# Cached decode attention with a gMLP gate: two blocks of w_out by three smaller transfers, and one group of chunks on a PSUM bank of its own

## The chip, the cores and the metric

One core of one Trainium2 chip. The metric is the device time of one execution in microseconds (us), the median of several runs.

## The reference

One decode step for 8 sequences with 512 features: an attention block over a cache of 4096 positions (32 query heads, 8 key/value heads of 128), multiplied by a gate from a gated MLP, added to the input.

```python
x = A_x                                   # [8, 1, 512]
xn = layernorm(x)
# attention: q = xn @ wq, softmax(q k^T / sqrt(128)) v over 4096 cached positions, then @ wo
s = A(xn, A_k_cache, A_v_cache, A_wq, A_wo)
# gMLP: z = gelu(xn @ w_in) [8, 1792]; z1, z2 = halves of 896; z2 = layernorm(z2)
#       g = w_sp * z2 + b_sp;  B = (z1 * g) @ w_out      (w_out is [896, 512])
g = silu(B(xn, B_w_in, B_w_sp, B_b_sp, B_w_out))
return x + s * g
```

All data are float32. The caches are 2 x 134 MB, so nearly all of the bytes are read once and used once.

## The kernel before

SBUF holds a ring of three slots of 8 MB (64 KB in each of 128 partitions). The first slot takes the MLP's weights (`mlp_slot`), the second `wq`, and from then on the slots take in turn the halves of the key cache (`load_k`, L295) and of the value cache (`load_v`, L302), one half per head, four sequences each. Every one of these loads is issued from the SP queue, in program order, and waits there until the slot that it overwrites has been read by TensorE. The last slot takes `wo` in seven pieces that get smaller (`WO_PIECES`, L319). So the SP queue holds the order: MLP weights (L62), extra w_out rows (L64), `wq` (L76), first half of the keys of head 0, second half of the keys of head 0 (into `mlp_slot`, so it waits for the MLP), then values, and so on.

The work on the engines goes in the same order. `mlp()` computes the gate at the start; `project_q` makes the queries; then, for each of 8 heads, `scores` (L240) for both halves, `softmax`, and `values` (L282) with `combine` (L291) for each sequence. At the end `wo` is multiplied (L333, L342), the gate applied, the input added, and the result stored.

In the MLP, w_in and w_out are cut into blocks of 128 rows. w_out has seven blocks. Five of them (`MAIN`) come with w_in in one transfer over all 128 partitions. The other two (`LOW`, blocks 1 and 3) come by a transfer of their own, `w_low`: each block is cut into 6 chunks of 24 rows (`CH` chunks of `QR` rows, the last chunk has 8), and the chunks lie in 24 partitions, 6 groups (`LOW_E`) of 4 rows (`LOW_R`). In DRAM each of the 6 groups is one stretch, followed by 64 numbers of padding, so that the transfer keeps an outer dimension of 6:

```python
nc.sync.dma_start(mlp_slot[:QR, n_mlp:n_low],
                  w_low[:, :LOW_R * N_LOW].rearrange("e (i n) -> e i n", n=N_LOW))
```

At the end of the MLP the product z1 * g (`u[:, 1]`) is transposed: two transposes of 128 columns for `MAIN` (L181, copied at L182 to `hT`), six of up to 24 columns for `LOW` (L188, copied at L192 to `hL`). Then 17 matmuls (L201; the profile has two records for each float32 matmul of this kind) multiply with the blocks and chunks of w_out. Matmul i goes to group i % 4 of 32 output partitions, all into one PSUM bank, `pw`. L202 copies it, L205 adds the four groups, and L207 to L211 make the gate. `xn`, the layer norm of the input, `hL`'s neighbour `hT` and the copy `y_sb` lie in small buffers; `xn` takes a part of `mlp_slot`.

Of the kernel before, what the change touches and what calls it, by code (L numbers as in the profile page):

```python
# [8 lines left out]
F32 = mybir.dt.float32  # L9
# [4 lines left out]
P = 128  # L14
B, D = 8, 512
HKV, REP, S, DH = 8, 4, 4096, 128
NK = D // P
G = 4
J = S // (G * P)
R = 32  # L20
FH = 896
FQ = 256
NB = FH // P
# [4 lines left out]
SLOT = HALF * UNIT  # L28
WO_PIECES = [(0, 8), (8, 16), (16, 24), (24, 28), (28, 30), (30, 31), (31, 32)]
FOLDED = 16  # L30
LOW_E, LOW_R = 6, 4
QR = LOW_E * LOW_R
CH = -(-P // QR)
MAIN = [0, 2, 4, 6, 5]
LOW = [1, 3]
N_LOW = len(LOW) * CH * D


@with_exitstack
def tile_gqa_gmlp_decode(ctx: ExitStack, tc: tile.TileContext, x, side, kT, v, wq, wo,  # L40
                         w_mlp, w_low, out):
    nc = tc.nc
    const = ctx.enter_context(tc.tile_pool(name="const", bufs=1))
    ring = ctx.enter_context(tc.tile_pool(name="ring", bufs=3))
    work = ctx.enter_context(tc.tile_pool(name="work", bufs=1))
# [4 lines left out]
    def slot():  # L50
        return ring.tile([P, SLOT], F32, name="slot")
# [6 lines left out]

    mlp_slot = slot()
    n_in, n_mlp = NK * 2 * FH, NK * 2 * FH + len(MAIN) * D  # L60
    n_low = n_mlp + N_LOW
    nc.sync.dma_start(mlp_slot[:, :n_mlp], w_mlp)  # L62
    w_in_sb = mlp_slot[:, :n_in].rearrange("p (k n) -> p k n", k=NK)
    nc.sync.dma_start(mlp_slot[:QR, n_mlp:n_low],  # L64
                      w_low[:, :LOW_R * N_LOW].rearrange("e (i n) -> e i n", n=N_LOW))
    w_out_sb = mlp_slot[:, n_in:n_mlp].rearrange("p (j d) -> p j d", d=D)
    w_low_sb = mlp_slot[:QR, n_mlp:n_low].rearrange("p (j a d) -> p j a d", a=CH, d=D)
    spare = [n_low]

    def from_slot(rows, n):  # L70
        lo = spare[0]
        spare[0] = lo + n
        return mlp_slot[:rows, lo:lo + n]
# [6 lines left out]
    ident = const.tile([P, P], F32, name="ident")  # L80
# [20 lines left out]
    sc = ps_fix.tile([P, 2, 512], F32, name="sc")  # L101
# [5 lines left out]
    def scratch(shape, name):  # L107
        t = ps.tile([P, 512], F32, name="scr")
        n = 1
        for s in shape[1:]:  # L110
            n *= s
        return t[:shape[0], :n]
# [2 lines left out]
    st = small.tile([B, 6], F32, name="st")  # L115
    mv = small.tile([B, 2], F32, name="mv")
    rstd = small.tile([B, 2], F32, name="rstd")
    xn = from_slot(B, D)
    nc.vector.bn_stats(st, x_sb)  # L119
    nc.vector.bn_aggr(mv, st)  # L120
    nc.vector.tensor_scalar(rstd[:, 0:1], mv[:, 1:2], EPS, None, op0=ALU.add)
# [9 lines left out]
    def mlp():  # L131
        zu = work.tile([P, 4, FQ], F32, name="zu", tag="p")
        z, u = zu[:, :2], zu[:, 2:]
        hy = work.tile([P, 2 * D], F32, name="hy", tag="pT")
        hT = hy[:, :2 * P].rearrange("p (a s) -> p a s", a=2)
        hL = hy[:QR, 2 * P:2 * P + CH * P].rearrange("p (a s) -> p a s", a=CH)
        y_sb, e = zu[:, :2].rearrange("p a f -> p (a f)"), zu[:, 2, :P]
        pz = scratch([P, 2 * FQ], "pz")
        nc.vector.memset(pz, 0.0)
        for part in range(2):  # L140
            for k in range(NK):
                for g in range(G):
                    lo = g * FQ
                    n = min(FQ, FH - lo)
                    nc.tensor.matmul(pz[R * g:R * (g + 1), part * FQ:part * FQ + n], xnT[:, k, :],  # L145
                                     w_in_sb[:, k, part * FH + lo:part * FH + lo + n],
                                     start=(k == 0), stop=(k == NK - 1))
        zf, uf = z.rearrange("p a f -> p (a f)"), u.rearrange("p a f -> p (a f)")
        nc.vector.tensor_copy(zf, pz)
        nc.vector.tensor_mul(uf, zf, zf)  # L150
        nc.vector.tensor_scalar(uf, uf, 0.044715, 1.0, op0=ALU.mult, op1=ALU.add)
        nc.vector.tensor_mul(uf, uf, zf)
        nc.scalar.activation(uf, uf, AF.Tanh, scale=GELU_C)
        nc.vector.tensor_scalar(uf, uf, 1.0, 0.5, op0=ALU.add, op1=ALU.mult)
        nc.vector.tensor_mul(zf, uf, zf)

        def mean(src, name):
            part_sum = small.tile([P, 1], F32, name="part_sum")
            nc.vector.tensor_reduce(part_sum, src, op=ALU.add, axis=AX.X)
            pm = scratch([P, 1], "pm")  # L160
            nc.tensor.matmul(pm, same_all, part_sum, start=True, stop=True)
            t = small.tile([P, 1], F32, name=name)
            nc.vector.tensor_scalar(t, pm, 1.0 / FH, None, op0=ALU.mult)
            return t

        z1, z2 = z[:, 0, :], z[:, 1, :]
        mu = mean(z2, "mu")
        nc.vector.tensor_scalar(z2, z2, mu, None, op0=ALU.subtract)
        nc.vector.tensor_mul(u[:, 0, :], z2, z2)
        nc.vector.memset(u[(G - 1) * R:, 0, FH - (G - 1) * FQ:], 0.0)  # L170
        var = mean(u[:, 0, :], "var")
        nc.vector.tensor_scalar(var, var, EPS, None, op0=ALU.add)
        rs = small.tile([P, 1], F32, name="rs")
        nc.gpsimd.tensor_tensor(rs, var, neg_half, op=ALU.pow)
        nc.vector.tensor_scalar(z2, z2, rs, None, op0=ALU.mult)
        nc.vector.tensor_scalar(z2, z2, side_sb[:, P:P + 1], side_sb[:, P + 1:P + 2],
                                op0=ALU.mult, op1=ALU.add)
        nc.vector.tensor_mul(u[:, 1, :], z2, z1)
        th = scratch([P, 2 * P], "th")
        for a in range(2):  # L180
            nc.tensor.transpose(th[:, a * P:(a + 1) * P], u[:, 1, a * P:(a + 1) * P], ident)  # L181
        nc.vector.tensor_copy(hT.rearrange("p a s -> p (a s)"), th)  # L182
        for lo in range(0, CH, 4):
            n = min(4, CH - lo)
            tl = scratch([QR, n * P], "tl")
            for a in range(lo, lo + n):
                k = min(QR, P - a * QR)
                nc.tensor.transpose(tl[:k, (a - lo) * P:(a - lo + 1) * P],  # L188
                                    u[:, 1, P + a * QR:P + a * QR + k], ident)
            for a in range(lo, lo + n):  # L190
                k = min(QR, P - a * QR)
                nc.vector.tensor_copy(hL[:k, a], tl[:k, (a - lo) * P:(a - lo + 1) * P])  # L192
        pw = scratch([P, D], "pw")
        todo = [(hT[:, j % 2, R * (j // 2):R * (j // 2 + 1)], w_out_sb[:, i, :]) for i, j in enumerate(MAIN)]
        for a in range(CH):
            k = min(QR, P - a * QR)
            todo += [(hL[:k, a, R * (j // 2):R * (j // 2 + 1)], w_low_sb[:k, i, a, :])
                     for i, j in enumerate(LOW)]
        for i, (lhsT, rhs) in enumerate(todo):
            g = i % G  # L200
            nc.tensor.matmul(pw[R * g:R * (g + 1), :], lhsT, rhs, start=(i < G), stop=(i + G >= len(todo)))  # L201
        nc.vector.tensor_copy(y_sb, pw)  # L202
        py = scratch([P, P], "py")
        for g in range(G):
            nc.tensor.matmul(py[R * g:R * (g + 1), :], same[:, 0, :], y_sb[:, g * P:(g + 1) * P],  # L205
                             start=True, stop=True)
        nc.vector.tensor_scalar(e, py, -1.0, 87.0, op0=ALU.mult, op1=ALU.min)  # L207
        nc.scalar.activation(e, e, AF.Exp)
        nc.vector.tensor_scalar(e, e, 1.0, None, op0=ALU.add)
        nc.vector.reciprocal(e, e)  # L210
        nc.vector.tensor_mul(gate, py, e)  # L211
# [86 lines left out]
    def load_v(h, half, parts):  # L298
# [4 lines left out]
        return t.rearrange("p (i j e) -> p i j e", i=HALF, j=J)  # L303

    mlp()
    project_q(0)
    project_q(1)
    for h in range(HKV):
        for half in range(2):
            scores(h, half, load_k(h, half))  # L310
        pT = softmax(h)
# [18 lines left out]
    part, acc = sc[:, 0, :], sc[:, 1, :P]  # L330
    for m in range(FOLDED):
        h, r = divmod(m, REP)
        nc.tensor.matmul(part[R * r:R * r + B, :], oT[:, h, r, :], wo_sb[:, m, :],  # L333
                         start=(m < REP), stop=(m >= FOLDED - REP))
# [11 lines left out]
    for g in range(G):  # L346
        nc.tensor.matmul(acc[R * g:R * g + B, :], same[:, 0, :B], part_sb[:, g * P:(g + 1) * P],
                         start=False, stop=False)
# [47 lines left out]
```

## Time and profile before

| what | value |
|---|---|
| median of 3 runs | 685.41 us (685.33 to 686.46) |
| the profiled execution | 685.31 us, its span 683.5 us |
| mean granted TensorE clock | 0.763 |
| DMA queue q1 (all loads of SP) | 6510 packets, 290.85 MB |
| HBM read | 290.87 MB, 426 GB/s over the span |

The profile is of one execution. The span runs from the first to the last instruction; the rest of the profiled execution's time lies around it. "DMA share" is the mean busy share of the core's 16 DMA engines; a row of windows gives it for a stretch of time, in microseconds from the span's start. In the chain of waits each row has a start, a length and what released the next. In groups and timeline, `out<-in` names what is written and read, x is a count, and the bracket says how long the engine was idle before and which instruction or transfer ended that.

### The profile page before, as it was taken

Reading aid. Unit: us, or ns where it says so; the run is one execution under the profiler, and the core shown is the slowest. Engines: PE = TensorE matmul, PEld = TensorE weight load, DVE = VectorE, ACT = ScalarE, POOL = GpSimd, SP = SyncE. Lnnn points to the kernel's source line nnn. Section 1 sums busy time; section 2 is a strip of 40 time slices with the busy share of each in tenths; the row PEclk is TensorE's granted clock in tenths of the full one; section 3 lists DMA queues with packets and bytes.
Section 4 is the critical chain, followed back from the end, with each engine's and each line's share of the span. In section 5 each row is a group of like instructions: output and inputs, shape, how many; then the busy total and the mean of one; then the engine's idle time right before and its main releaser. Section 6 shows DMA issues by size and latency. Waiting matters only on the chain.

```text
span 683.5 us, 5757 instructions
## 1 busy us (share of the span) xinstructions
PE 373.0 (55%) x2634; PEld 115.1 (17%) x2634; DVE 168.0 (25%) x272; ACT 13.5 (2%) x27; POOL 3.9 (1%) x11
## 2 busy tenths in 40 slices
PE   1486454446665455556754454555754455645665
PEld 0221121112111111111211021111211121111222
DVE  2420032402430023401431024401422024400350
ACT  0000000000000000000000000000000000000000
POOL 1000000000000000000000000000000000000000
PEclk9778777767778777777787767767777777777788
DMA  9999999999999999999999999999999999999995
GB/s 396 438 430 427 430 442 426 438 433 434 433 427 445 430 433 433 427 427 433 430 437 430 437 430 434 430 430 433 430 430 438 430 434 437 434 430 438 404 427 238
DMA packets 6693, 291.29 MB, mean 426 GB/s; under 512 B 750, under 2 KB 1006, under 8 KB 1398
## 3 DMA queue, kind: packets, MB, share of 16 engines
q1 hardware_dynamic: 6510, 290.85, 98.7%
q8 instruction: 20, 0.33, 0.2%
q10 hardware_dynamic: 160, 0.08, 0.1%
q14 instruction: 3, 0.02, 0.0%
HBM read 290.87 MB, written 0.07 MB: 426 GB/s over the span
## 4 chain that ended last, share of the span: by engine, by line
DMA 80%; PE 15%; issue 4%; DVE 1%; SPq 0%; POOLq 0%; POOL 0%
DMA slot<-in_kT 41%; DMA slot<-in_v 35%; PE sc L240 8%; PE o_ps L282 5%; DMA slot<-in_wo 4%; PE scr L201 1%; PE po_ps L291 0%; DMA x_sb<-in_x 0%; DVE o_sb L287 0%; PE scr L188 0%; SPq L302 0%; DVE hy L192 0%; DVE o_all L285 0%; DVE st L119 0%; PE scr L181 0%
## 5 line engine op out<-in xcount | busy, mean ns | idle before, releaser
L240 PE MATMUL sc<-slot,qz 128*32 128x512 f32 x1024 | 144.1, 726 | 136.1 <-DMA slot<-in_kT 136.1
L282 PE MATMUL o_ps<-slot,pT 128*16 128x512 f32 x1024 | 151.0, 730 | 79.2 <-DMA slot<-in_v 79.2
L285 DVE TENSOR_TENSOR o_all<-o_ps,diag 128x512 f32<-128x512 f32 x64 | 44.3, 692 | 154.2 <-PE o_ps L282 153.7
L245 DVE TENSOR_REDUCE nm<-sc 128x1 f32<-128x1024 f32 x8 | 9.8, 1225 | 278.7 <-PE sc L240 278.7
L240 PEld LDWEIGHTS sc<-slot,qz 128*32 128x32 f32 x1024 | 35.5, 131 | 238.3 <-DMA slot<-in_kT 139.5
L287 DVE TENSOR_REDUCE o_sb<-o_all 128x128 f32<-128x512 f32 x64 | 67.7, 1059 | 2.2
L282 PEld LDWEIGHTS o_ps<-slot,pT 128*16 128x16 f32 x1024 | 29.5, 111 | 159.0 <-issue 108.2
L291 PE MATMUL po_ps<-fold,o_sb 128*128 128x4 f32 x128 | 24.9, 264 | 27.7 <-DVE o_sb L287 27.5
L291 PEld LDWEIGHTS po_ps<-fold,o_sb 128*128 128x128 f32 x128 | 19.2, 189 | 72.5 <-DVE o_sb L287 72.5
L271 PE MATMUL scr<-ident,p 128*128 128x128 f32 x64 | 14.8, 410 | 10.7 <-DVE p L266 10.7
L247 ACT ACTIVATE p<-sc,nm 128x1024 f32<-128x1024 f32 x8 | 8.9, 1114 | 577.4 <-DVE nm L245 577.4
L271 PEld LDWEIGHTS scr<-ident,p 128*128 128x128 f32 x64 | 11.9, 212 | 11.1 <-issue 11.1
L272 DVE COPY pT<-scr 128x512 f32<-128x512 f32 x16 | 11.1, 692 | 10.8 <-PE scr L271 10.8
L145 PE MATMUL scr<-slot,xnT 128*32 128x256 f32 (+1 forms) x64 | 6.4, 547 | 9.6 <-DMA slot<-in_w_mlp 9.6
L218 PE MATMUL scr<-slot,xnT 128*32 128x512 f32 x64 | 8.6, 684 | 0.0
L250 PE MATMUL scr<-ident,nm 128*1 128x128 f32 x8 | 2.2, 270 | 10.9 <-DVE nm L245 10.9
L263 PE MATMUL scr<-wl,same 128*128 128x1 f32 x16 | 3.2, 272 | 6.2 <-DVE wl L261 6.2
L201 PE MATMUL scr<-slot,hy 24*32 24x512 f32 (+2 forms) x34 | 6.2, 726 | 0.5 <-DVE hy L192 0.5
L342 PE MATMUL sc<-slot,oT 128*8 128x128 f32 x128 | 4.4, 273 | 3.8 <-DMA slot<-in_wo 3.8
L266 DVE TENSOR_SCALAR p<-p,w 128x1024 f32<-128x1024 f32 x8 | 6.0, 753 | 0.3
L145 PEld LDWEIGHTS scr<-slot,xnT 128*32 128x32 f32 x64 | 3.4, 161 | 12.2 <-issue 12.1
L333 PE MATMUL sc<-slot,oT 128*8 128x512 f32 x32 | 5.2, 785 | 0.0
(84 smaller groups left out, 62.8 us busy)
## 6 DMA issues: line engine op xcount, KB each, us to landing
slot<-in_v SPq DMA_DIRECT2D x4, 2048.0 KB, 41.9
slot<-in_wo SPq DMA_DIRECT2D x3, 2048.0 KB, 41.5
slot<-in_w_mlp SPq DMA_DIRECT2D x1, 4864.0 KB, 14.6
slot<-in_wo SPq DMA_DIRECT2D x1, 1024.0 KB
slot<-in_w_low SPq DMA_DIRECT2D x1, 576.0 KB
slot<-in_wo SPq DMA_DIRECT2D x1, 512.0 KB, 33.1
slot<-in_wo SPq DMA_DIRECT2D x2, 256.0 KB, 26.7
slot<-in_kT SPq DMA_DIRECT2D x16, 48.5
```

The source lines that it names most:

```text
L145: nc.tensor.matmul(pz[R * g:R * (g + 1), part * FQ:part * FQ + n], xnT[:, k, :], w_in_sb[:, k, part * FH + lo:part * FH + lo + n], start=( ...
L201: nc.tensor.matmul(pw[R * g:R * (g + 1), :], lhsT, rhs, start=(i < G), stop=(i + G >= len(todo)))
L218: nc.tensor.matmul(pq[R * g:R * (g + 1), :], xnT[:, k, :], wq_sb[:, k, lo:lo + REP * DH], start=(k == 0), stop=(k == NK - 1))
L240: nc.tensor.matmul(sc[R * g:R * (g + 1), c, :], qz[:, h, b * R:(b + 1) * R], k_sb[:, i, c, g, :], start=(b == 0), stop=(b == B - 1))
L245: nc.vector.tensor_reduce(m, sc, op=ALU.max, axis=AX.XY, negate=True)
L247: nc.scalar.activation(p.rearrange("p j s -> p (j s)"), sc.rearrange("p c s -> p (c s)"), AF.Exp, bias=m, accum_out=l[:, h:h + 1])
L271: nc.tensor.transpose(t[:, j * P:(j + 1) * P], p[:, 4 * c + j, :], ident)
L272: nc.vector.tensor_copy(pT[:, :, 4 * c:4 * c + 4].rearrange("p b j (g r) -> p (j g) b r", g=G), t.rearrange("p (m b r) -> p m b r", b=B, r ...
L282: nc.tensor.matmul(of[R * c:R * c + G * REP, :], pT[:, b, j, :], v_unit[:, j], start=(j < G), stop=(j >= J - G))
L285: nc.vector.tensor_mul(o_all, o, diag[:, :, None].to_broadcast([P, G, DH]))
L287: nc.vector.tensor_reduce(o_sb, o_all.rearrange("p g d -> p d g"), op=ALU.add, axis=AX.X)
L291: nc.tensor.matmul(po[:, b * REP:(b + 1) * REP], o_sb, fold, start=True, stop=True)
```

## The change

The two blocks of `LOW` are cut in another way, and come by three transfers in place of one. Each entry of `LOW` is now: groups of 4 rows, first partition, first column behind the other MLP weights, and the chunks (block, first row).

- 2 groups at partitions 32 to 39: the first 64 rows of block 3 in 8 chunks of 8 rows.
- 4 groups at partitions 0 to 15: all of block 1 in 8 chunks of 16 rows.
- 8 groups at partitions 0 to 31: the last 64 rows of block 3 in 2 chunks of 32 rows.

Each transfer has a DRAM tensor of its own with the same padding of 64 numbers behind each group. The transposes follow the chunks: 18 for `LOW` in place of 6, with one copy for up to four chunks of equal height. The matmuls whose chunks lie at partition 32 (the 8-row ones) accumulate in a PSUM bank of their own: `sc[:, 1]`, while the five of `MAIN` and the ten other chunks use `sc[:, 0]`; `sc` is the score tile, which is free at that time. The second bank is added to the copy of the first. `hL` moves into `mlp_slot`, and `xn` moves out of it into a work buffer.

```diff
-LOW_E, LOW_R = 6, 4
-QR = LOW_E * LOW_R
-CH = -(-P // QR)
+LOW_R = 4
 MAIN = [0, 2, 4, 6, 5]
-LOW = [1, 3]
-N_LOW = len(LOW) * CH * D
+def rows_of(j, lo, hi, n):
+    return [(j, r) for r in range(lo, hi, n)]
+LOW = [(2, R, 2 * D, rows_of(3, 0, P // 2, 8)), (4, 0, 2 * D, rows_of(1, 0, P, 16)),
+       (8, 0, 0, rows_of(3, P // 2, P, 32))]
+LOW_COLS = 10 * D
+HL_AT = [0, 0, 8]
+HL_CH = 10
...
-    nc.sync.dma_start(mlp_slot[:QR, n_mlp:n_low],
-                      w_low[:, :LOW_R * N_LOW].rearrange("e (i n) -> e i n", n=N_LOW))
+    low_sb = []
+    for (e, p0, c0, chunks), w_low in zip(LOW, lows):
+        t = mlp_slot[p0:p0 + e * LOW_R, n_mlp + c0:n_mlp + c0 + len(chunks) * D]
+        nc.sync.dma_start(t, w_low[:, :LOW_R * len(chunks) * D].rearrange("e (i n) -> e i n", i=LOW_R))
+        low_sb.append(t.rearrange("p (c d) -> p c d", d=D))
...
-    xn = from_slot(B, D)
+    xn = work.tile([B, D], F32, name="xn", tag="pT")
...
-        hL = hy[:QR, 2 * P:2 * P + CH * P].rearrange("p (a s) -> p a s", a=CH)
+        hL = from_slot(P, HL_CH * P).rearrange("p (a s) -> p a s", s=P)
...
-        for lo in range(0, CH, 4):
-            n = min(4, CH - lo)
-            tl = scratch([QR, n * P], "tl")
-            for a in range(lo, lo + n):
-                k = min(QR, P - a * QR)
-                nc.tensor.transpose(tl[:k, (a - lo) * P:(a - lo + 1) * P],
-                                    u[:, 1, P + a * QR:P + a * QR + k], ident)
-            for a in range(lo, lo + n):
-                k = min(QR, P - a * QR)
-                nc.vector.tensor_copy(hL[:k, a], tl[:k, (a - lo) * P:(a - lo + 1) * P])
-        pw = scratch([P, D], "pw")
...
-        for i, (lhsT, rhs) in enumerate(todo):
-            g = i % G
-            nc.tensor.matmul(pw[R * g:R * (g + 1), :], lhsT, rhs, start=(i < G), stop=(i + G >= len(todo)))
-        nc.vector.tensor_copy(y_sb, pw)
+        todo = [(0, hT[:, j % 2, R * (j // 2):R * (j // 2 + 1)], w_out_sb[:, i, :]) for i, j in enumerate(MAIN)]
+        for (ne, p0, _, chunks), c0, w_low in zip(LOW, HL_AT, low_sb):
+            n = ne * LOW_R
+            for lo in range(0, len(chunks), 4):
+                some = chunks[lo:lo + 4]
+                rows = [min(n, P - r) for j, r in some]
+                tl = scratch([n, len(some) * P], "tl")
+                for i, (j, r) in enumerate(some):
+                    nc.tensor.transpose(tl[:rows[i], i * P:(i + 1) * P], u[:, 1, P + r:P + r + rows[i]], ident)
+                for i, (j, r) in enumerate(some):
+                    if i and rows[i] == rows[0]:
+                        continue
+                    m = rows.count(rows[i])
+                    nc.vector.tensor_copy(
+                        hL[p0:p0 + rows[i], c0 + lo + i:c0 + lo + i + m].rearrange("p a s -> p (a s)"),
+                        tl[:rows[i], i * P:(i + m) * P])
+                todo += [(int(p0 > 0), hL[p0:p0 + rows[i], c0 + lo + i, R * (j // 2):R * (j // 2 + 1)],
+                          w_low[:rows[i], lo + i, :]) for i, (j, r) in enumerate(some)]
+        for bank in range(2):
+            part = [(lhsT, rhs) for k, lhsT, rhs in todo if k == bank]
+            for i, (lhsT, rhs) in enumerate(part):
+                g = i % G
+                nc.tensor.matmul(sc[R * g:R * (g + 1), bank, :], lhsT, rhs,
+                                 start=(i < G), stop=(i + G >= len(part)))
+            if bank == 0:
+                nc.vector.tensor_copy(y_sb, sc[:, 0, :])
+            elif part:
+                nc.vector.tensor_add(y_sb, y_sb, sc[:, 1, :])
```

## The prediction

> **What bounds the kernel now.** I read the head of the page first, then its DMA rows, then the chain that ended last.
>
> ```profile
> span 683.5 us, 5757 instructions
> PE 373.0 (55%) x2634; PEld 115.1 (17%) x2634; DVE 168.0 (25%) x272; ACT 13.5 (2%) x27; POOL 3.9 (1%) x11
> ...
> DMA  9999999999999999999999999999999999999995
> ...
> q1 hardware_dynamic: 6510, 290.85, 98.7%
> q8 instruction: 20, 0.33, 0.2%
> ...
> DMA 80%; PE 15%; issue 4%; DVE 1%; SPq 0%; POOLq 0%; POOL 0%
> ...
> slot<-in_w_low SPq DMA_DIRECT2D x1, 576.0 KB
> ```
>
> The 16 DMA engines are busy from end to end (9 in every slice but the last), and 290.85 MB go through queue q1, which SP alone feeds. No compute engine is above 55%. So a change in the MLP at the start counts only through the bytes that each DMA engine carries, or if it ever leaves a DMA engine without a queued transfer. The next question is how evenly the 16 engines end. The windows over the last microseconds show it, with the end of the chain beside them.
>
> ```profile
> 655.46 24.52 DMA slot<-in_wo
> 679.99 0.04 issue
> 680.03 0.45 PE sc L342 x8
> ```
> ```profile
> core 0: us, PE busy (x) PEld busy (x) DVE busy (x) ACT busy (x) POOL busy (x), PEclk, DMA share, GB/s
> 672.00:673.00 1.00, 0.00 (x0) 0.00 (x0) 0.69 (x1) 0.00 (x0) 0.00 (x0) 1.00 0.91 373
> 673.50:676.00 2.50, 0.93 (x36) 0.96 (x40) 0.00 (x0) 0.00 (x0) 0.00 (x0) 1.00 0.78 315
> 676.20:676.40 0.20, 0.20 (x19) 0.20 (x10) 0.00 (x0) 0.00 (x0) 0.00 (x0) 1.00 0.63 246
> 676.50:677.00 0.50, 0.50 (x28) 0.43 (x16) 0.00 (x0) 0.00 (x0) 0.00 (x0) 1.00 0.55 197
> 677.30:677.80 0.50, 0.34 (x14) 0.34 (x18) 0.00 (x0) 0.00 (x0) 0.00 (x0) 1.00 0.15 57
> 677.95:678.90 0.95, 0.75 (x32) 0.46 (x24) 0.00 (x0) 0.00 (x0) 0.00 (x0) 1.00 0.10 37
> 679.00:679.90 0.90, 0.75 (x23) 0.17 (x12) 0.00 (x0) 0.00 (x0) 0.00 (x0) 1.00 0.03 11
> ```
>
> The column before the last is the mean busy share of the 16 engines; one engine kept busy would be 0.06. The share falls in steps: a few engines are done at 673.5, most end between 676.2 and 677.8, and in the last 2 us only one or two still work (0.10, then 0.03, less than one engine's full share because the last pieces are small). PE's last eight matmuls start at 680.03, when the last byte has landed at 679.99. So the time is set by the **slowest single DMA engine**. About 14 of the 16 are done some 2.2 us before it.
>
> **The change, part by part.** The kernel before puts two of the seven w_out blocks into a transfer of 6 groups of 4 rows, 576 KB, which I take to be 96 KB on each of six engines (0 to 5, a group each), beside the rest that all 16 share alike. The trace has no engine numbers; this is read from the shape of the transfer. The change sends the same two blocks as 2 groups x 4 rows x 16 KB, 4 groups x 4 rows x 16 KB and 8 groups x 4 rows x 4 KB. If a group is an engine's share and the numbering starts anew with each transfer, engines 0 and 1 get 64+64+16 = 144 KB, engines 2 and 3 64+16 = 80 KB, engines 4 to 7 16 KB, the rest nothing; 512 KB in all.
>
> The rate of one engine comes from a stretch in which all are busy:
>
> ```profile
> 15.10:18.00 2.90, 2.57 (x27) 1.55 (x30) 0.00 (x0) 0.00 (x0) 0.00 (x0) 1.00 1.00 429
> ```
>
> 429 GB/s over 16 is 26.8 GB/s. Then 96 KB take 3.67 us, 144 KB 5.50, 80 KB 3.06, 16 KB 0.61. Against before, engines 0 and 1 end 1.83 us later, 2 and 3 end 0.61 earlier, 4 and 5 end 3.06 earlier, 6 and 7 end 0.61 later, 8 to 15 where they did. Nothing later evens this out: every further transfer gives all 16 the same, and the queues do not run dry in between, so the difference is carried to 680 us. That the extra rows set the late group fits the picture: 3.67 us is about the distance from the first step of the staircase (673 to 673.5) to the bulk.
>
> The second source of unevenness is q8: 20 packets of 0.33 MB in all, 16 KB each, which took 0.2% of 16 x 683.5 us, 22 us, so 1.1 us of one engine's time per packet. Twenty do not divide evenly by 16; an engine that took two more than another ends some 2 us later, the size of the tail behind the bulk. The page "Runtime: NRT & Kernel Launch" of the Trainium skill, Instruction fetch mechanics, says that instructions are refilled in 16 KiB blocks of 256. The trace agrees: 2 x 2634 records of PE by 256 are 20.6. The change adds 12 transposes and 6 matmuls (12 records), each with its weight load: 48 records, 0.2 of a block, so at most one more packet. On the last engine it costs 1.1 us, on another nothing; I take nothing.
>
> **The MLP's tail** grows, and must stay hidden. Its rows:
>
> ```profile
> 33.05 0.87 PE scr L188 x4
> ...
> 34.87 6.27 PE scr L201 x34
> 41.15 36.29 DMA slot<-in_kT
> ```
> ```profile
> 1.17 0.93 SPq L64 DMA_DIRECT2D slot<-in_w_low  x1
> 2.14 0.40 SPq L76 DMA_DIRECT2D slot<-in_wq  x1
> ...
> 33.94 1.27 DVE L192 COPY hy<-scr 24x128 f32<-24x128 f32 x6 [0.43 <-PE scr L188]
> ...
> 41.16 0.69 DVE L202 COPY zu<-scr 128x512 f32<-128x512 f32 x1 [5.95 <-PE scr L201]
> ...
> 58.22 8.95 PE L240 MATMUL sc<-slot,qz 128*32 128x512 f32 x64 [4.44 <-DMA slot<-in_kT]
> ```
> ```profile
> SPq L295 <- PE scr L201: 22.3, 1, 22.3
> ```
>
> Transposes: 18 for 6, 12 more at 0.87/4 = 0.22 us are 2.6 us. Copies: four of 512 columns and one of 256 for six of 128; at 0.69 us for 512 that is 3.1 us for 1.27, 1.8 more if nothing overlaps. Matmuls: 46 records for 34, 12 more at 6.27/34 = 0.18 us are 2.2 us. One addition of about 0.7 us follows the second bank, behind the last read of the slot. So L201's successor ends between 2.2 us (transposes and copies overlapped) and 6.6 us later, at 43.4 to 47.8 in place of 41.15. The second kT load is what waits for it (22.3 us, SP). It is needed when the fastest engine has worked off the first kT. That load was complete at 58.2 on the slowest engine; the staircase at the end is about 7 us wide, so the fastest had it no earlier than 51. That leaves 3 us at the least and nearer 6, and the cost is nothing; were that cover gone, each microsecond would cost one. Behind the MLP, query projection and first scores start up to 7.3 us later (the addition counts here). The first scores would run at 59 to 66 and not at 58.2, their slot's reload is needed only after two more transfers of 19 us, and nothing else is queued.
>
> The **two added DMA issues** on SP are 0.93 us each at most, which moves wq from 2.14 to about 4.0, long before the engines finish the MLP weights at 14. The move of the layer-norm output to another buffer and of hL into the slot: nothing, the same operations. Small packets: the third transfer's 4 KB rows cost 0.15 us each by the rate above and, if each had a fixed part, perhaps twice that, 1.2 us for the four of an engine in place of 0.61; no row shows one alone; I take the first, and the other end would put 0.6 us on the end, within the forecast's own range.
>
> The Trainium skill's "DMA: Bandwidth & Descriptors", Measured and Anatomy of one DMA, speaks against small transfers: about 2.0 us fixed for each. By it two more would cost 4 us. That sentence is about one transfer waited for by itself. Here the share is 1.00 in the window quoted above, where the small transfer and its successor follow the weights: queued transfers leave no hole. I keep it as a rival below.
>
> **The sum** stands against the profiled execution: 685.31 us, of which the span is 683.5 and 1.8 lies around it; the median of the three runs is 685.41, 0.1 above. The end moves by the latest of: the old last engine's shift, engines 0 and 1 where they stand plus 1.83, and the others. If engines 0 and 1 are in the bulk (676.2 to 677.8), they end at 678.0 to 679.6; if the last engine is 2 or 3 it ends at 679.4, if 4 or 5 at 676.9. So the end is 678.0 to 679.6 in place of 680.0, in the middle about 679.1: 0.9 us less, **684.4 us**, with 683.3 to 684.9 as that case's own range.
>
> **The rivals.** No view tells which of the six engines are the last two, so the cases go by where they stand.
>
> First, *the last engine is 0 or 1* (it gets 1.83 us on top): 680.0 becomes 681.8, 687.1 us. It decides if that one engine is in the pair, one in three by place alone, provided it is one of the six at all; if it is an engine above 7, the change can bring nothing, and engines 0 and 1 decide only above 678.2. For it: nothing spares the low engines from instruction packets. Against: nothing names them. Chance 0.30.
>
> Second, *the second last is in the pair* and the last is not: the share of 0.10 until 678.9 puts it at about 679, plus 1.83 is 680.8, 686.2 us. One in four; chance 0.23.
>
> Third, *the groups do not steer*: if every transfer is spread over all engines, or numbering goes round and does not start anew, only 64 KB less move, 0.15 us by 429 GB/s: 685.2 us. Against it stands the staircase, which an even spread of w_low would not give so clearly. Chance 0.03. The fixed cost per transfer, on the path, gives 685.3 - 0.9 + 4 = 688.4; against it the share of 1.00. Chance 0.01. The *MLP's tail* running past the fastest engine's queue needs over 10 us of growth before it passes 51, where the sum has 6.6 at most: 0.02, at about 686.
>
> **How the numbers follow.** The forecast's case has the rest, 0.41, the likeliest. What a measurement of this kernel can tell from no change is about 0.2%, 1.4 us. Of the 0.41, about half lies beyond it (an end at 678.6 or before): 0.21 faster. Slower by more: the first rival, 0.30, the fixed cost, and a little of the second and of the tail: 0.34. Within it: the rest of the forecast's case, most of the second rival, the third: 0.45. The range reaches from 683.7 to 687.3, to hold the first two rivals, and leaves out the best end of the forecast and the rarer cases. Its own case alone would be 683.3 to 684.9.
>
> **What would show it.** Right: in the last windows the share falls below 0.2 later than 677.3 (engines 0 and 1 moved up), and the end of in_wo comes at 678.6 to 679.6; DMA moves 0.07 MB less. First rival: the share of one engine persists to 681.8, and PE's last matmuls start there. Tail: the row of L201's successor ends before 48 and the wait of SP for it is under 30 us; a first kT window (51 to 58 us) with a DMA share under 0.9 would show a queue run dry. Transposes should be 18 and the records of the w_out matmuls 46. A q8 count of 21 would be the added instruction packet. Wrong altogether: a hole in the DMA row of the page, or an end that is off with the staircase unchanged.

## The result, and the profile after

The changed kernel takes 684.36 us in the median of ten runs (684.15 to 684.55). The kernel before, beside it, took 686.66 us (685.23 to 687.91, ten runs). The ratio is 0.997 with a 95% interval of 0.996 to 0.998: faster by 0.3%. The forecast was 684.4 us with a range of 683.7 to 687.3. The time is met to 0.04 us, yet the likeliest verdict of the forecast, "within 0.2%", is not: the kernel before is slower in most executions than in the one whose profile the forecast was worked from. Both halves are taken up below.

The page of the profiled execution after (684.55 us, span 682.7):

```profile
span 682.7 us, 5811 instructions
PE 379.3 (56%) x2658; PEld 116.7 (17%) x2658; DVE 170.5 (25%) x272; ACT 13.5 (2%) x27; POOL 3.9 (1%) x11
...
q1 hardware_dynamic: 6550, 290.79, 98.8%
q8 instruction: 21, 0.34, 0.2%
```

24 records more on PE and as many weight loads, 0.06 MB less on q1, and a 21st instruction packet on q8. The end of the chain, and the same windows over the last microseconds as before:

```profile
654.32 24.59 DMA slot<-in_wo
678.96 0.45 PE sc L358 x8
```
```profile
core 0: us, PE busy (x) PEld busy (x) DVE busy (x) ACT busy (x) POOL busy (x), PEclk, DMA share, GB/s
672.00:673.00 1.00, 0.00 (x0) 0.00 (x0) 0.00 (x0) 0.00 (x0) 0.00 (x0) 1.00 0.92 377
673.50:676.00 2.50, 1.97 (x72) 1.89 (x72) 0.00 (x0) 0.00 (x0) 0.00 (x0) 1.00 0.77 310
676.20:676.40 0.20, 0.00 (x1) 0.01 (x1) 0.00 (x0) 0.00 (x0) 0.00 (x0) 1.00 0.55 215
676.50:677.00 0.50, 0.50 (x24) 0.50 (x22) 0.00 (x0) 0.00 (x0) 0.00 (x0) 1.00 0.52 201
677.30:677.80 0.50, 0.31 (x16) 0.15 (x12) 0.00 (x0) 0.00 (x0) 0.00 (x0) 1.00 0.33 123
677.95:678.90 0.95, 0.73 (x20) 0.15 (x12) 0.00 (x0) 0.00 (x0) 0.00 (x0) 1.00 0.07 26
679.00:679.90 0.90, 0.36 (x8) 0.07 (x8) 0.43 (x2) 0.00 (x0) 0.00 (x0) 1.00 0.07 18
```

PE's last matmuls start at 678.96 in place of 680.03. Between 677.3 and 677.8 the share is 0.33 where it was 0.15: more engines end late, and none ends as late as the last one did. (The 0.07 of the last row is the 21st instruction packet, 16 KB begun at 679.3, after the last piece of wo has landed.) The share hides which engine is which. The packet records and semaphore updates of the trace give more: for each transfer, when each of its DMA engines completed. For the last piece of wo, in microseconds after the first engine (which completes at 673.1 to 673.2 in all of these profiles; rows two, four and five are runs told below):

```
before           0.00 0.19 0.23 3.00 3.22 3.48 3.53 3.59 3.77 4.13 4.54 4.57 4.62 4.69 5.73 6.76
before, 3rd      0.00 0.04 0.37 3.13 3.28 3.28 3.37 3.51 3.51 3.62 3.74 4.37 4.76 4.87 5.91 8.33
after            0.00 0.70 0.71 1.56 3.22 3.45 3.53 3.82 4.25 4.74 4.85 5.01 5.29 5.55 5.65 5.83
eight groups     0.00 0.31 2.31 2.45 2.70 2.71 3.12 3.17 3.21 3.47 3.74 4.57 4.59 4.69 5.80 7.15
five and two     0.00 0.02 0.52 3.16 3.28 3.32 3.34 3.37 3.62 4.48 4.70 4.72 4.78 5.09 5.10 5.42
```

The right-hand column sets the time. The trace has no engine numbers; an engine is followed by its distance from the first, which stays the same within about 0.1 us from one transfer to the next unless something delays it. Followed back in this way, the last two engines after (5.65 and 5.83) are the two of the 2-group transfer: they are 5.67 and 5.87 behind when wq completes at 34 us and hold that distance to the end, so no instruction packet delays them here. The last engine before is one of the six of w_low, 3.7 behind at the start, with two steps of about 1.55 us on the way.

The tail of the MLP, in the timeline after:

```profile
1.17 2.25 SPq L73 DMA_DIRECT2D slot<-in_w_low  x3
...
42.76 2.15 PE L213 MATMUL sc<-slot 8*32 8x512 f32 x16 [0.79 <-DVE zu L216]
44.95 0.33 SPq L311 DMA_DIRECT2D slot<-in_kT  x1
44.96 0.69 DVE L218 TENSOR_TENSOR zu<-zu,sc 128x512 f32<-128x512 f32 x1 [2.25 <-PE sc L213]
```

It ends 3.8 us later (44.95 for 41.15), and the second load of keys is issued then. The fastest engine completes the first load at 53.2, 8 us later, and the first engine completes the second load 19.35 us after that, eight packets of 2.42, so nothing ran dry.

### The profile page after: what moved, and what is told of

Read it like the earlier page. It is cut to its first block, busy times and chain, and to the rows that moved or that the text cites. A ratio compares the mean times of both kernels' runs of the same rounds, so it can differ in the third digit from the quotient of the medians.

```text
span 682.7 us, 5811 instructions
## 1 busy us (share of the span) xinstructions
PE 379.3 (56%) x2658; PEld 116.7 (17%) x2658; DVE 170.5 (25%) x272; ACT 13.5 (2%) x27; POOL 3.9 (1%) x11
## 4 chain that ended last, share of the span: by engine, by line
DMA 79%; PE 14%; issue 4%; DVE 2%; SPq 0%; POOLq 0%; POOL 0%
DMA slot<-in_kT 41%; DMA slot<-in_v 35%; PE sc L256 8%; PE o_ps L298 4%; DMA slot<-in_wo 4%; PE sc L213 1%; DVE o_sb L303 1%; PE scr L199 1%; PE po_ps L307 0%; DVE o_all L301 0%; DMA x_sb<-in_x 0%; SPq L318 0%; DVE zu L216 0%; DVE st L127 0%; PE scr L189 0%
## 5 line engine op out<-in xcount | busy, mean ns | idle before, releaser
L298 PE MATMUL o_ps<-slot,pT 128*16 128x512 f32 x1024 | 153.1, 739 | 75.6 <-DMA slot<-in_v 75.6
L213 PE MATMUL sc<-slot 16*32 16x512 f32 (+2 forms) x36 | 4.9, 617 | 0.8 <-DVE zu L216 0.8
```

The source lines that it names most:

```text
L213: nc.tensor.matmul(sc[R * g:R * (g + 1), bank, :], lhsT, rhs, start=(i < G), stop=(i + G >= len(part)))
L298: nc.tensor.matmul(of[R * c:R * c + G * REP, :], pT[:, b, j, :], v_unit[:, j], start=(j < G), stop=(j >= J - G))
```

## The experiments

Placement theory: the time is the end of the slowest DMA engine; the groups of a transfer choose the lowest-numbered engines; instruction packets go to some of the engines only. Rivals: only the bytes count (bytes theory); or the rearranged MLP brought the gain (tail theory).

**The old split in the new code.**

```diff
-LOW = [(2, R, 2 * D, rows_of(3, 0, P // 2, 8)), (4, 0, 2 * D, rows_of(1, 0, P, 16)),
-       (8, 0, 0, rows_of(3, P // 2, P, 32))]
+LOW = [(6, 0, 0, rows_of(1, 0, P, 24) + rows_of(3, 0, P, 24))]
...
```

(hL keeps 32 columns for each chunk there, to fit.)

> The changed kernel's code with the split of before: six groups of 24-row chunks in one transfer (96 KB on each of six DMA engines), one PSUM bank. Placement theory (the time is the end of the slowest DMA engine, and groups choose the lowest-numbered engines): back at the times of before, 685.2 to 687.9 us, with a single late engine among the six. Bytes theory (only the 64 KB less that the change loads count): 684.5. Tail theory (the other order of the MLP's tail, xn and hL in other buffers, brought the gain): 684.4, as the changed kernel.

685.76 us (685.24 to 686.86, 12 runs); against before 0.9994 (0.9984 to 1.0004). The new code with the old split is the old kernel. The tail theory falls. The number that I wrote for the bytes theory was mis-worked: this kernel loads the old bytes, so that theory expects the old time too. It can explain 0.15 us of the gain at most (64 KB by 430 GB/s).

**The same bytes on eight engines.** `LOW = [(8, 0, 0, rows_of(1, 0, P, 32) + rows_of(3, 0, P, 32))]`, one bank.

> The same 512 KB as the changed kernel in one transfer of 8 groups of 32-row chunks, 64 KB (2.4 us) on each of engines 0 to 7, one bank. Placement theory, if the instruction packets of q8 go round engines 5 to 12 as the traces suggest: engines 5, 6 and 7 carry 2.4 us and two or three instruction packets of 1.5 us each, so they end 1 us later or more than the last engine now: 684.8 to 686.3 us, and it scatters between runs. Bytes theory: 684.4, as the changed kernel, since the bytes are the same.

684.42 us (684.12 to 686.11, 12 runs), in two clusters: seven runs at 684.1 to 684.4, five at 685.6 to 686.1. The median is below what I expected and the scatter is as expected. The profile (685.58 us; the fourth row of the table) shows why: of the eight engines that carry 64 KB only two are delayed by instruction packets, not three; one of them took two packets (5.80) and one three (7.15). The seven early runs, of which there is no profile, fit two packets on both. So the changed kernel's split is not better than this one at its best; it is rid of the bad runs.

**64 KB more on engines 0 and 1.**

```diff
+    nc.sync.dma_start(mlp_slot[40:48, n_mlp + 2 * D:n_mlp + 10 * D],
+                      lows[0][:, :LOW_R * 8 * D].rearrange("e (i n) -> e i n", i=LOW_R))
```

> The changed kernel with its 2-group transfer issued a second time, into free space (64 KB more on each of two engines, 128 KB in all; the copy is not used). Placement theory: engines 0 and 1 end the kernel, so all of it shows: 4 packets of 0.61 us, 2.4 us more, 686.8 us. Bytes theory (the bytes are shared by all 16 engines): 128 KB by 430 GB/s, 0.3 us more, 684.7.

689.44 us (689.16 to 689.67, 6 runs): 5.1 us more, twice the placement theory's 2.4 and far from the bytes theory's 0.3. In the trace six of the eight added 16 KB packets took 1.27 to 1.29 us each where those of w_low took 0.61, and 30 packets of wq on other engines, beside them, took 2.6 to 4.8 us in place of 2.42:

```profile
18.50:24.00 5.50, 2.95 (x33) 1.39 (x27) 2.38 (x4) 0.00 (x0) 0.00 (x0) 1.00 1.15 319
```

The same window of the changed kernel has 429 GB/s:

```profile
18.50:24.00 5.50, 3.20 (x41) 1.49 (x33) 2.13 (x4) 0.00 (x0) 0.00 (x0) 0.99 0.99 429
```

All engines lost 2.5 us (the first completes wq at 36.3, not 33.8), and engines 0 and 1 took another 2.2 to 2.3 there. The copy went to partitions 40 to 47. That made the place in SBUF a suspect, which the next run isolates.

**Other partitions, nothing else.** `LOW = [(2, 2 * R, ...` in place of `(2, R, ...`: the 8-row chunks at partition 64.

> The changed kernel with the 2-group transfer (and its part of hL) at partitions 64 to 71 in place of 32 to 39; bytes, engines and instructions are the same. If it matters into which partitions an engine writes, and partitions 32 to 39 belong to engines 0 and 1 in the full transfers while 64 to 71 belong to engines 8 and 9: the packets of 16 KB take about 1.27 us and not 0.61, those of wq beside them 3.5 to 4.8 and not 2.42 us, and the end is 2.5 us later, 686.9 us (the 4.9 us that the doubled transfer cost, less 2.4 for its bytes). If the place does not matter, and the doubled transfer was slow for another reason: 684.4 us.

686.88 us (686.58 to 687.15, 10 runs), 2.5 us over the changed kernel; the ratio to before is 1.0006 (0.9997 to 1.0015): the whole gain is gone. Its 16 KB packets took 1.25 to 1.34 us while they overlapped with others, packets of wq up to 4.9 us, and the first engine completes wq at 36.5, 2.7 us later. So the "partition 32" of this change matters as much as the split. "SBUF — State Buffer" in the Trainium skill, Door 1: the DMA port swizzle, says that partitions 32 apart share a port and 64 apart do not. The Trainium skill's "DMA: Bandwidth & Descriptors", The descriptor swizzle, gives partitions 0 to 3 and 32 to 35 to engine 0 in a transfer over all 128 partitions. The trace agrees: at 32 the small packets run at 0.61 us, at 40 and 64 most of them at twice that. No view names a port, so the port as the cause is the Trainium skill's word; that the place alone costs 2.5 us is measured.

**A flatter split.**

```diff
+LOW = [(2, R, 0, rows_of(1, 120, P, 8) + rows_of(3, 80, P, 8)),
+       (5, 0, 0, rows_of(1, 0, 120, 20) + rows_of(3, 0, 80, 20))]
...
```

> The same 512 KB as 5 groups of ten 20-row chunks and 2 groups of seven 8-row chunks: 136 KB on engines 0 and 1, 80 KB on 2, 3 and 4, nothing above 4. Placement theory: engines 0 and 1 end 0.3 us earlier and the engines with instruction packets above 4 lose their 16 KB, so 684.0 to 684.1 us. Bytes theory: 684.4, no difference to the changed kernel.

684.10 us (683.92 to 684.18, 7 runs; the changed kernel had 684.15 to 684.55): 0.26 us better, as small as expected, and against before 0.9968 (0.9955 to 0.9981). The two were not measured side by side, and the fastest run of the kernel before differs by 0.15 us from one such occasion to another; the firmer sign is the last engine's 5.42 for 5.83 in the table. It is the best version here. Its chain ends at

```profile
678.62 0.45 PE sc L358 x8
```

None of the five marked engines took an instruction packet of q8. One lost about 1 us twice, when packets of q14 passed (a second queue of instruction packets, three in the span). What is left to gain is little: the last row of the table has seven engines between 4.5 and 5.4, four of them unmarked, out of the reach of a low-numbered group.

**Eight more instruction packets.** 16 small matmuls after each `scores` and each half of the values.

> The changed kernel with 512 small matmuls more on TensorE (16 in each pass over half of the keys or values; their results are not used), 2048 records, about eight instruction packets more on q8, one on each engine that q8 visits. Placement theory: engines 0 and 1 take no such packets and end as before, but the engine that now ends 0.3 us ahead of them and takes three packets gets a fourth of 1.5 us: end 1.0 to 1.3 us later, 685.4 to 685.7 us. Bytes theory: 131 KB by 430 GB/s, 0.3 us, 684.7. A theory that TensorE's work is on the path would give up to 25 us, the length of the added matmuls.

685.61 us (685.05 to 685.99, 11 runs), 1.25 us more, as expected. Records on PE rise by 2 x 1024, and the page has

```profile
q8 instruction: 29, 0.48, 0.3%
```

against 21. The last engine is at 6.94 in the count of the table, which four packets of 1.55 us make on a start 0.7 behind the first. PE at 65% busy costs nothing by itself.

**A longer tail of the MLP.** 16 or 34 multiplications by 1 ahead of the transposes.

> The changed kernel with 16 multiplications by 1 ahead of the transposes of the MLP, 5.8 us more. The prediction's cover: the second load of keys is issued at 50.7 and not at 44.95 us, still before the fastest engine has worked off the first at 53.2: no change, 684.4 us. If the tail's growth costs already: up to 5.8 us more, 690.

> The same with 34 multiplications, 12.2 us more: the load is issued at 57.2, 4 us after the fastest engines ran dry, but before engines 0 and 1 do (59.1). Then all engines but these two start again together near 58.4 and take their two or three instruction packets (3.1 to 4.7 us) afterwards: end 3 to 4 us later, 687.4 to 688.4 us. If the cover were wider than predicted: 684.4. If each microsecond past 53.2 cost one for the slowest engine: 689.5.

684.67 us (684.46 to 684.95, 6 runs) and 688.27 us (687.58 to 689.00, 10 runs). The second is as expected. The first is 0.3 us more by the medians, though the ranges overlap, and its trace shows a small loss. The issue of its load ends at 50.8, 2.4 us before the first engine is through with the load ahead, and the first engine completes it at 73.3 and not 72.5. By the packet records the load's first packets begin up to about half a microsecond late, and most take 2.6 to 3.7 us for 2.42. With 34 multiplications the engines do stand. The stretch behind 53.2, in the changed kernel and in that one:

```profile
53.50:55.00 1.50, 1.50 (x18) 0.46 (x20) 0.49 (x4) 0.00 (x0) 0.00 (x0) 1.00 0.61 262
```
```profile
53.50:55.00 1.50, 1.45 (x16) 0.40 (x16) 0.00 (x0) 0.00 (x0) 0.00 (x0) 0.95 0.31 131
```

A row counts a packet where it begins, and a packet of 64 KB takes 2.42 us, so in a row of 1.5 us the 0.61 of the changed kernel is no idle time. Up to 56.9 us, 22 such packets begin in the changed kernel and 6 in the other: most engines stand. The tail of the change can grow by some 5 us more before it costs. Counted from the kernel before that is some 9 us, where the rival named over 10.

**Which engines q8 visits.** A transfer of 13 groups, to mark engines 0 to 12.

```diff
+    nc.sync.dma_start(mlp_slot[64:116, n_mlp:n_mlp + 4 * D],
+                      lows[len(LOW)][:, :LOW_R * 4 * D].rearrange("e (i n) -> e i n", i=LOW_R))
...
```

> The changed kernel with one more small transfer of 13 groups of 4 rows, 32 KB (1.2 us) on each (zeros, not used): it marks engines 0 to 12 in the packets of the trace. If q8 goes round engines 5 to 12, every engine that is delayed by an instruction packet is a marked one, and the three unmarked stay ahead to the end by the marked ones' 1.2 us and more; the time is 685.6 us, as engines 0 and 1 end 1.2 us later. If q8 visits engines 13 to 15 too, an unmarked engine falls behind by 1.5 us in steps.

689.21 us, 3.6 us over the expectation: it lies at partitions 64 to 115, most of them not those of its engines, and slows the others as above. Of the three unmarked engines two fell behind by 1.55 us when packets of q8 passed at 204 and 229 us, so "5 to 12" is wrong. With the other runs, each by its lowest-numbered engines: none of 0 to 4 (five groups) is visited, one of 0 to 5 (six groups), two of 0 to 7 (eight groups), and two of the last three. In the profiles that I followed through, q8 goes round eight engines in one order: 5, one of 6 and 7, four of 8 to 12, two of 13 to 15.

**The kernel before again.** Two more profiles of it.

> The kernel before, for a second profile of it. Its executions have spans of 683.4 to 684.0 us or of 684.9 to 685.5 us. If the long ones are those in which the last DMA engine takes three instruction packets of q8 and not two, a long profile shows the last engine 1.5 us behind where it was in the first profile, all others unchanged but for the phase of the round; a short one looks like the first profile.

> The same, a third profile of the kernel before; the same two pictures, by the length of its span.

The second profile has a span of 683.6 us and the picture of the first; the time is 686.08, 2.48 us above its span. The third has 685.0 us (time 687.07), and the picture that was asked for: the same engine of the six steps from 3.69 to 5.22 by 53 us, to 6.77 by 305 and to 8.34 by 595, three packets in place of two (second row of the table). In its windows one engine is busy past 680:

```profile
679.00:679.90 0.90, 0.90 (x32) 0.70 (x32) 0.00 (x0) 0.00 (x0) 0.00 (x0) 1.00 0.07 27
680.10:681.40 1.30, 1.03 (x24) 0.45 (x24) 0.00 (x0) 0.00 (x0) 0.00 (x0) 1.00 0.04 16
```

Of 70 further runs of the kernel before, 41 had spans of 683.4 to 684.0 us and 29 of 684.9 to 685.5. The round starts elsewhere in each execution (engine 5 was the seventh to be visited in the first profile, the first in the third), and 20 packets give a third one to four of the eight. Three packets are seen in the one profile with a long span, and two are seen in the four profiles of this split with a short span; for the 70 runs it goes by the span.

**48 records more in the kernel before.** The time outlasts the span by 1.73 to 3.28 us in those 70 runs, by over 2.0 in 30. In the profile of the six-group variant (time 686.37, span 683.4) a packet comes after the last instruction; the view of DMA from 684.5 to 687 us shows nothing else:

```profile
q8 instruction: 1, 0.02, 3.5%
```

```diff
+        d = scratch([R, 1], "d")
+        for _ in range(12):
+            nc.tensor.matmul(d, same[:, 0, :], diag[:, 0:1], start=True, stop=True)
```

> The kernel before with 12 small matmuls more in the MLP (48 records on TensorE, as many as the change adds; results not used). If the 1 to 1.5 us by which many executions of the kernel before outlast their span are an instruction packet fetched after the last instruction, as in the profile of the six-group variant, these 48 records move that packet into the span: time less span is 1.7 to 2.0 us in all runs. The spans stay where they are, 683.4 to 684.0 or 684.9 to 685.5 us, as the DMA engines' loads are those of before. If the excess has to do with something else of the split: it stays, up to 3.3 us.

685.48 us in the median (685.34 to 687.15, 12 runs). Time less span is 1.73 to 1.90 us in all twelve, and the spans are still of two kinds, 683.6 to 683.7 (seven) and 685.0 to 685.4 (five). The changed kernel, with its 48 records, has 1.73 to 1.95. The eight-group variant, with 12 records fewer than the kernel before, has 1.73 to 1.84 as well: only a narrow range of lengths is hit. That part of the gain is an accident of where a block of instructions ends. (By the ratio of all runs, 0.9994 with 0.9983 to 1.0004, this gain alone cannot be told from none.)

## Why the prediction was right, and where not

*The bound* was right: the slowest DMA engine. Rates of engines, loads by groups and lowest numbers hold: engines 0 and 1 were 5.7 to 5.9 us behind at 34 us, 5.50 by the sum; the rest is within the 0.8 us by which the ten engines outside w_low differ at that point before. That numbers start anew with each transfer was shown by no row of before. It follows from the Trainium skill's "DMA: Bandwidth & Descriptors", Why a DMA increments its semaphore by 16 and not by 1: a transfer whose descriptors are made in hardware (HWDGE, as those that SP issues) runs on the lowest-numbered engines. The trace agrees, since the distances add.

*The staircase* was read half rightly. Its bulk is not the late group of w_low alone: by the distances of before, four of the six engines of w_low stand there, and seven others came there by two or three instruction packets each: two make 3.1 us, which looks like the 3.67 of w_low.

*The case* that I held likeliest came true: the heavy pair stood in the bulk. They ended at 678.7 and 678.9, inside 678.0 to 679.6; the chain ends 1.07 us earlier, for a forecast of 0.9. The late engine was number 5, which lost 80 KB. No view at hand showed where the pair stood, and the case had a chance of 0.41, so that the time is met to 0.04 us is in part luck.

*The tail* ended at 44.95, inside 43.4 to 47.8; SP waited 25 us for it (20.0 and 5.2 in two rows), under the 30 named. Costing it at nothing was right, and the rival's cover of over 10 us was nearly so (some 9). *The rows of 4 KB* took 0.159 us for 0.15. *A fixed 2 us per transfer* is not there: one, two and three transfers (eight groups at its best, five and two, the change) are within 0.3 us of each other. The 2.0 us of the Trainium skill's "DMA: Bandwidth & Descriptors", Anatomy of one DMA, is given there for transfers that GpSimd issues; these come from SP.

*What failed* is the step "the sum stands against the profiled execution", with the chances that hang on it. I took 685.31 us, 0.1 from the median of three runs, as the kernel's level, and left the run at 686.46 aside. The level is a mixture, and two terms were missing. An instruction packet costs its engine about 1.55 us, not the 1.1 that its own time gave, since the data packet beside it is stretched too (2.9 to 3.0 us for 2.42); and I asked how many such packets there are, but not whether the last engine gets the same number each time. It takes two or three: 1.5 us in 29 of 70 runs. And one packet after the last instruction adds up to 1.5 us in 30 of 70. The change moved the end to engines that q8 does not visit, and pushed that last packet into the span. The 22 of the 70 runs with a short span and less than 2.0 us around it have a median of 685.44, 1.1 above the changed kernel. So 1 us of the 2.3 between the medians is what was forecast, and the rest is the disappearance of bad executions. "Faster by over 0.2%" deserved more than 0.21.

*The rivals.* The pair as the last engine (0.30) was a fair risk by what the profile showed, but in no profile here does q8 delay one of engines 0 to 4. The second last engine of before (5.73) is one of the six of w_low as well, and so the second rival (0.23) was a real one: it starts 3.9 behind and is delayed by 1 us twice, when packets of q14 pass at 54 and 406 us. After the change the engine so delayed is one of the two with 80 KB, 2 or 3, and not one of the pair: it starts 3.4 behind and ends at 5.29. The 21st packet was foreseen, and cost nothing: it came behind the last piece of wo.

## What to carry to other kernels

Where one queue keeps all DMA engines busy, the time is the end of the slowest one, so look at how the DMA share falls in the last microseconds, and place small transfers by their number of groups on the engines that end early. Take several runs before calling a level: a spread with two clusters can have a mechanism, as here, and a placement that avoids it can be worth more than the median of a few runs shows. Keep each group in the partitions that its engine fills in full-width transfers, and give a small transfer's place as much care as its size.

## What the runs showed of the hardware

- Instruction packets of TensorE (16 KB, q8) go round eight of the sixteen DMA engines in a fixed order from a starting point that differs by execution, and each delays its engine by about 1.55 us: its own 1.0 to 1.1, and a data packet stretched from 2.42 to 2.9 to 3.0.
- Writing 128 KB from two DMA engines into partitions other than their own doubled most of those packets (1.25 to 1.34 us for 0.61) and stretched 64 KB packets of other engines from 2.42 to as much as 4.9 us; it cost 2.5 us at the end.
- A load whose issue ended 2.4 us before the first engine was through with the load ahead came too late: the first engine completed it 0.8 us later than otherwise.
